# Batch 7 and the last tail with two weighted numerators, batch 1 loaded as fp32, and a new order

## The chip, the cores and the metric

The kernel runs on one core of one Trainium2 chip. The metric is the device time of one execution in microseconds (us). Before the change it is 264.87 us (median of three runs, 264.82 to 264.91). In the text PE is TensorE, DVE is VectorE, ACT is ScalarE, POOL is GpSimd and SP is SyncE; SP only issues transfers (DMAs) here.

## The reference

Attention with a feature map, then a gated MLP with a mixing over positions. There are 8 batches, 8 heads, 576 positions, a head size of 64 and 128 features. Cut to what matters:

```python
def phi(x):                                   # x: q or k, per head
    proj = x @ w_phi                          # 64 -> 128 features
    proj = proj - max(abs(proj), axis=-1)     # m, one number per position and head
    return concat([exp(proj), exp(-proj)])    # 256 features
q_p, k_p = phi(q), phi(k)
num = q_p @ (k_p.T @ v)                       # per batch and head
den = q_p @ k_p.sum(positions) + 1e-6
x   = (num / den)                             # heads side by side: 512 columns
h    = relu(x @ w_in)                         # 512 -> 1024, halves u and v
v_n  = (v - mean(v)) / sqrt(var(v) + 1e-6)    # over the 512 columns
v_s  = w_spatial @ v_n + b_spatial            # over the 576 positions
out  = (u * v_s) @ w_out                      # 512 -> 512
```

As the code has it, the subtraction of m stands ahead of both exponentials: the first half of the features is exp(p - m) and the second is exp(-(p - m)), which is exp(-p + m).

## The kernel before

**Tiling.** Of a batch's 576 positions, 512 are four blocks of 128 and 64 are left over: the tail. The tails of two batches are worked together, as group g for batches 2g and 2g+1. The query side of a batch falls into four units, each of 256 positions and four heads (names with `b.cc.hg`: batch, pair of position blocks, half of the heads); a tail group is one more unit.

**The key side.** k is turned on PE or by a transposing transfer, multiplied by w_phi (`kp`, line 578), DVE takes the maxima of the magnitudes (`km`, line 583), ACT takes both exponentials (`ke`, line 587) and those of the maxima (`kem`, line 592), POOL scales v by them (`vs`, line 633), and PE sums keys times scaled values (`kv`, lines 663 and 665). DVE or ACT copies the sums to SBUF (`kvc`).

**The query side, per unit.** PE multiplies q by w_phi by position (`qp`, line 578); DVE takes the maxima (`qm`, line 583); POOL splits them into two bf16 numbers (`qs`, lines 678 and 679); PE turns them (`qt`, line 683); ACT or DVE copies them (`qc`). Then `qf` makes the features by column: two wide products (line 689), and eight products with a constant `sel` that subtract the maxima in PSUM (line 693). ACT takes exp(p) and exp(-p) of the result (`qe`, line 698). `qn` (line 748) makes 16 short products of 66 columns: both halves of the features accumulate into one sum, whose last columns hold the denominator. DVE takes the reciprocal (`qr`, line 754) and multiplies (`qx`, line 759) into x. The tail's names end in t.

**The MLP.** x is turned (by a transposing transfer `xx` or by PE, `tx`), `vm` and `um` multiply by the two halves of w_in (lines 853 and 921), `vr` and `ur` rectify, `vb` and `va` take mean and variance on DVE, POOL normalizes (`vn`), `sm` mixes positions (lines 935 and 937), `sg` gates on DVE (line 944), `om` multiplies by w_out (line 950), `oc` copies to SBUF and `od` sends the result out.

**The order.** A long string, `ORDER`, lists every step with its engine (`@A` ACT, `@V` DVE, `@P` POOL, `@S` SP, none for PE) and its buffer or PSUM bank numbers. The program is written out in this order, and each engine runs its instructions in it. `warm.n` is n products of the identity (line 365) whose result nobody reads. Batch 0's q and k are loaded as fp32 by SP and ACT and turned on PE; from batch 1 on POOL issues the loads (`lk`, `lq`, lines 398 and 402), which cast to bf16. The functions that would load batch 1 as fp32 (`lkg`, `lqg`) exist, and the list does not use them.

## Time and profile before

The profiled execution took 264.64 us; its span, from the first to the last instruction, is 262.8 us.

| what | us | of the span |
|---|---|---|
| PE busy (weight loads run beside it, 164.0) | 250.8 | 95% |
| DVE busy | 206.6 | 79% |
| ACT busy | 202.2 | 77% |
| POOL busy | 185.1 | 70% |
| first product by w_v starts at | 48.1 | |
| last product by w_out ends, and the last padding starts, at | 258.2 | |
| mean granted clock of TensorE | 1.000 | |

A row of the groups reads: line, engine, operation, tile written and tiles read, shapes, count, then total busy time and the mean duration of one in ns, then the engine's idle time just before them and what ended it. In a table by stage each engine has its busy time in that stretch and, in brackets, the instructions in it. Durations of neighbours on an engine overlap a little, and those of PE a lot: a matmul's row ends long after the next has started.

### The profile page before, as it was taken

To read this page: it belongs to the slowest core of one execution; us is meant where nothing else is said; L and a number is where in the kernel's file an instruction comes from. 1 tells how busy PE (TensorE), PEld (TensorE's weight loads), DVE (VectorE), ACT (ScalarE), POOL (GpSimd) and SP (SyncE) were. 2 spreads that over 40 slices of the span, in tenths; PEclk is the share of its full clock that TensorE was granted. 3 is DMA by queue.
4 is the path that set the end of the run, shared out by engine and by line. 5 is a ranking of instruction groups with operands and counts; after the bars stand their busy time and mean duration, and the time that the engine had idled before them with its cause. 6 is when DMAs were issued, how large, how long until landed. Compare 5 with 4: busy or idle time off the path is not lost.

```text
span 262.8 us, 8513 instructions
## 1 busy us (share of the span) xinstructions
PE 250.8 (95%) x3464; PEld 164.0 (62%) x3499; DVE 206.6 (79%) x362; ACT 202.2 (77%) x330; POOL 185.1 (70%) x338
## 2 busy tenths in 40 slices
PE   7999989999999998989999999999999999999993
PEld 7978768666566565666665766555547586446441
DVE  0679889998899898798899877999987848655730
ACT  3689989999769999999999896997899762453032
POOL 8627996999997996687999992369989820288000
PEclk9999999999999999999999999999999999999999
DMA  7999999962797979998999999998630130044045
GB/s 196 305 193 296 192 203 230 234 75 42 198 209 164 193 123 141 209 143 87 208 205 197 225 107 144 212 197 209 178 127 2 40 84 8 36 159 162 11 148 203
DMA packets 80090, 41.35 MB, mean 157 GB/s; under 512 B 48946, under 2 KB 75442, under 8 KB 80052
## 3 DMA queue, kind: packets, MB, share of 16 engines
q1 hardware_dynamic: 58628, 29.93, 53.1%
q0 software_dynamic: 20592, 10.10, 33.2%
q10 hardware_dynamic: 832, 0.79, 0.9%
q8 instruction: 27, 0.44, 0.7%
q14 instruction: 11, 0.09, 0.1%
HBM read 32.82 MB, written 9.44 MB: 161 GB/s over the span
## 4 chain that ended last, share of the span: by engine, by line
PE 67%; POOL 19%; DVE 5%; DMA 4%; issue 3%; ACT 0%; POOLq 0%; DVEq 0%; ACTq 0%
PE banks L853 10%; PE banks L950 9%; PE banks L935 9%; PE banks L921 8%; POOL vs L633 5%; PE banks L748 5%; PE banks L578 4%; PE banks L663 4%; DMA ld<-in_q_dram 4%; DVE mq L583 3%; PE banks L689 3%; POOL vn L863 2%; POOL vst L645 2%; PE banks L937 2%; PE banks L693 2%
## 5 line engine op out<-in xcount | busy, mean ns | idle before, releaser
L698 ACT ACTIVATE qf<-banks 128x1024 bf16<-128x1024 f32 x72 | 70.1, 1030 | 6.0 <-PE banks L693 5.5
L587 ACT ACTIVATE kf<-banks 128x1024 bf16<-128x1024 f32 x64 | 63.9, 1037 | 5.2 <-PE banks L578 4.8
L633 POOL TENSOR_TENSOR vs<-v,em 128x512 bf16<-128x512 f32 x64 | 65.7, 1043 | 3.0 <-ACT em L592 2.8
L583 DVE TENSOR_REDUCE mq<-banks 128x8 f32<-128x1024 f32 x36 | 43.4, 1220 | 4.1 <-PE banks L578 2.5
L583 DVE TENSOR_REDUCE mk<-banks 128x8 f32<-128x1024 f32 x32 | 38.8, 1218 | 4.5 <-ACT kf L587 2.4
L921 PE MATMUL banks<-xT,w_u 128*128 128x512 bf16 x128 | 32.3, 380 | 0.0
L935 PE MATMUL banks<-w_spT,vn 128*128 128x512 bf16 x116 | 31.6, 379 | 0.7 <-issue 0.2
L853 PE MATMUL banks<-w_v,xT 128*128 128x512 bf16 x118 | 31.2, 379 | 0.5
L950 PE MATMUL banks<-w_out,uT 128*128 128x512 bf16 x113 | 29.6, 379 | 0.7 <-issue 0.2
L277 ACT COPY ob<-banks 128x512 f32<-128x512 f32 x23 | 13.5, 597 | 19.4 <-PE banks L950 18.7
L944 DVE TENSOR_TENSOR uT<-banks,uT 128x512 bf16<-128x512 f32 x32 | 21.4, 683 | 6.4 <-PE banks L937 6.1
L863 POOL TENSOR_SCALAR vn<-vr,mv,rs 128x512 bf16<-128x512 bf16 x32 | 24.4, 767 | 1.2
L663 PEld LDWEIGHTS <-kf 128*128 128x128 bf16 x512 | 21.9, 97 | 4.3 <-issue 0.8
L663 PE MATMUL banks<-vs,kf 128*128 128x66 bf16 x512 | 23.9, 194 | 0.5 <-POOL vs L633 0.3
L875 DVE BATCH_NORM_STATS2 st<-vr 128x6 f32<-128x512 bf16 x32 | 21.5, 683 | 3.5 <-ACT vr L283 3.2
L578 PE MATMUL banks<-wphi,T 64*128 64x128 bf16 x512 | 22.8, 217 | 0.4
L759 DVE TENSOR_TENSOR x<-banks,rc 128x512 bf16<-128x512 f32 x32 | 22.1, 690 | 0.9
L283 ACT ACTIVATE vr<-banks 128x512 bf16<-128x512 f32 (+1 forms) x28 | 16.8, 606 | 7.3 <-PE banks L853 5.8
L748 PEld LDWEIGHTS <-qf 128*128 128x128 bf16 x512 | 19.2, 98 | 4.4 <-issue 0.9
L365 PE MATMUL banks<-ident 128*128 128x128 bf16 x237 | 19.4, 234 | 2.1 <-POOL ident L279 1.7
L665 PE MATMUL banks<-vst,kft 128*128 128x66 bf16 x128 | 21.1, 191 | 0.1
L748 PE MATMUL banks<-kv,qf 128*128 128x66 bf16 x512 | 21.0, 193 | 0.0
(123 smaller groups left out, 481.2 us busy)
## 6 DMA issues: line engine op xcount, KB each, us to landing
v<-in_v_dram SPq DMA_DIRECT2D x16, 512.0 KB, 6.9
out_dram<-ob SPq DMA_DIRECT2D x31, 256.0 KB, 3.0
ld<-in_q_dram POOLq DMA_DIRECT2D x7, 512.0 KB, 10.8
ld<-in_k_dram POOLq DMA_DIRECT2D x7, 512.0 KB, 10.4
uT<-in_q_dram SPq DMA_DIRECT2D x2, 512.0 KB, 5.3
vt<-in_v_dram SPq DMA_DIRECT2D x8, 128.0 KB, 8.6
out_dram<-ob SPq DMA_DIRECT2D x8, 128.0 KB, 3.3
vn<-in_moe_w_spatial_dram POOLq DMA_DIRECT2D x1, 576.0 KB, 7.8
```

What stands on the lines that cost most here:

```text
L578: nc.tensor.matmul(out=bank(banks[y])[:, n * F:(n + 1) * F], lhsT=xT[halves[y], n, :], rhs=wphi[halves[y], :], start=True, stop=True)
L583: nc.vector.tensor_reduce(out=out_, in_=pp.rearrange("p y (n f) -> p y n f", f=F), axis=AX.X, op=ALU.max, apply_absolute_value=True)
L587: nc.scalar.activation(out=kf[:, s].rearrange("p y n f -> p y (n f)"), in_=pp, func=AF.Exp, bias=0.0, scale=(1.0, -1.0)[s])
L633: ENG[e].tensor_tensor(out=get("vs", (b, j))[:, s, :, 0:D], in0=at["v", (b, j // 2)][:, (j % 2) * n:(j % 2 + 1) * n, :], in1=at["em", (b, ...
L663: nc.tensor.matmul(out=pv[:, hh, s, :], lhsT=kf[:, s, c % 2, 2 * hh + c // 2, :], rhs=w[:, s, NB * hh + c, :], start=(c == 0), stop=False)
L698: nc.scalar.activation(out=at["qf", u][:, s].rearrange("p y n t -> p y (n t)"), in_=at["pq", u], func=AF.Exp, bias=0.0, scale=(1.0, -1.0)[s])
L748: nc.tensor.matmul(out=at["pn", u][:, y, n, :], lhsT=f[:, s, y, n, :], rhs=at["kv", b][:, hg * HH + n, s, :], start=(s == 0), stop=(s == 1))
L853: nc.tensor.matmul(out=bank(place)[r], lhsT=lhs[:, kc, r], rhs=w_v[:, kc, :], start=(kc == 0), stop=(kc == KC - 1))
L863: ENG[e].tensor_scalar(out=out_, in0=in_, scalar1=mv, scalar2=rs, op0=ALU.add, op1=ALU.mult)
L921: nc.tensor.matmul(out=bank(place).rearrange("p (c t) -> p c t", c=NB), lhsT=w_u[:, kc, dc * P:(dc + 1) * P], rhs=at["xT", b][:, :, kc, :] ...
L935: nc.tensor.matmul(out=bank(place), lhsT=at["vn", b][:, c, cs], rhs=w_spT[:, c, 0:T0], start=(c == 0), stop=False)
L950: nc.tensor.matmul(out=bank(place), lhsT=at["uT", b][:, dc, c * P:(c + 1) * P], rhs=w_out[:, dc, :], start=(dc == 0), stop=(dc == KC - 1))
```

## The change

Three things change.

- **Batch 7's four units and the last tail group.** The products `qg` are those of `qf` without the eight subtractions, so the exponentials are exp(p) and exp(-p) of the plain projection. `qna` and `qnb` make the sums of either half on its own, in PSUM banks of their own. ACT computes exp(-2m) from the maxima (`qw`), DVE weights the first sum by it (`qy`) and adds the second (`qz`), both over 528 values, and takes the reciprocal from SBUF (`qv`); POOL multiplies into x (`qu`). Numerator and denominator have one common factor less, exp(m), which cancels but for the 1e-6. `qs`, `qt`, `qc`, `qf`, `qn`, `qr` and `qx` of these units go.
- **Batch 1's q and k** are loaded by SP as fp32 (`lkg`, `lqg`, into tiles that the MLP uses later) instead of by POOL as bf16, and its 32 transposes on PE read fp32. The fp32 copy of w_phi now lies in a tile of x.
- **The list `ORDER`** is another one throughout: order, buffer and bank numbers, which engine does a copy or a rectification, and the padding, 237 products before and 211 after.

```diff
-BUFS = dict(ld=3, T=7, ..., mT=4,
+BUFS = dict(ld=3, T=7, ..., mT=4, wq=6, tq=1,
...
+        wq=([P, 2, HH], FP32),
+        tq=([P, 2, HH, DA], FP32),
...
-    wphi_f = const("wphi_f", [D, F], FP32)
+    wphi_f = buf["x"][0][0:D].rearrange("p a h d -> p (a h d)").bitcast(FP32)[:, 0:F]
...
+    def features_u(u, xT):
+        banks = [places.pop(0), places.pop(0)]
+        for y in range(2):
+            nc.tensor.matmul(out=bank(banks[y]).rearrange("p (n t) -> p n t", n=HH), lhsT=wphi[halves[y], :],
+                             rhs=xT[halves[y]], start=True, stop=True)
+        at["pq", u] = pair(*banks)
+
+    def weight(u):
+        nc.scalar.activation(out=get("wq", u), in_=at["mq", u], func=AF.Exp, bias=0.0, scale=-2.0)
...
+    def half_sums(b, cc, hg, s):
+        u = (b, cc, hg)
+        f = at["qf", u]
+        pn = at["pn", u, s] = sums((places.pop(0), places.pop(0)))
+        for y in range(2):
+            for n in range(HH):
+                nc.tensor.matmul(out=pn[:, y, n, :], lhsT=f[:, s, y, n, :], rhs=at["kv", b][:, hg * HH + n, s, :],
+                                 start=True, stop=True)
...
+    def weigh(u, w, r=slice(0, P)):
+        nc.vector.tensor_tensor(out=get("tq", u)[r], in0=at["pn", u, 0][r],
+                                in1=at["wq", w][r].unsqueeze(3).to_broadcast([r.stop - r.start, 2, HH, DA]), op=ALU.mult)
+
+    def join(u, r=slice(0, P)):
+        t = at["tq", u][r]
+        nc.vector.tensor_tensor(out=t, in0=at["pn", u, 1][r], in1=t, op=ALU.add)
+
+    def inverse(u, r=slice(0, P)):
+        nc.vector.reciprocal(out=get("rc", u)[r], in_=at["tq", u][r, :, :, D:D + 1])
+
+    def divide(e, out_, u, r=slice(0, P)):
+        ENG[e].tensor_tensor(out=out_, in0=at["tq", u][r, :, :, 0:D],
+                             in1=at["rc", u][r].to_broadcast([r.stop - r.start, 2, HH, D]), op=ALU.mult)
```

Three places show how the list moves instructions. First, SP's queue from its start; `ob` takes k of batch 0, `uT` its q, `tf` and `vt` the tails, `v` the values, and in the new list `vn` and `xT` take k and q of batch 1. Before:

```order
L382 DMA ob_164<-in_k_dram 128x2x256
L293 DMA tf_77<-in_k_dram 64x8x64 x2
L318 DMA wphi_f<-in_w_phi_dram 64x128
L386 DMA uT_159<-in_q_dram 128x4x256
L386 DMA uT_160<-in_q_dram 128x4x256
L382 DMA ob_166<-in_k_dram 128x2x256
L406 DMA v_75<-in_v_dram 128x4x256
L293 DMA tf_78<-in_q_dram 64x8x64 x2
L293 DMA vt_80<-in_v_dram 64x8x64 x2
L406 DMA v_73<-in_v_dram 128x4x256
```

After:

```order
L385 DMA ob_173<-in_k_dram 128x2x256
L321 DMA x_132<-in_w_phi_dram 64x128
L389 DMA uT_166<-in_q_dram 128x4x256
L389 DMA uT_167<-in_q_dram 128x4x256
L296 DMA tf_78<-in_k_dram 64x8x64 x2
L409 DMA v_72<-in_v_dram 128x4x256
L393 DMA vn_163<-in_k_dram 128x4x256
L393 DMA vn_161<-in_k_dram 128x4x256
L397 DMA xT_137<-in_q_dram 128x4x256
L296 DMA tf_77<-in_q_dram 64x8x64 x2
L296 DMA vt_80<-in_v_dram 64x8x64 x2
L397 DMA xT_136<-in_q_dram 128x4x256
```

Four loads of batch 1 now stand among those of batch 0; the second piece of v (`v_73`) comes after them.

Second, DVE about the first gating products of batch 0, where `TENSOR_SCALAR` is a rectification, `TENSOR_REDUCE` a maximum and `uT` the u half of the MLP. Before:

```order
L754 RECIPROCAL rc_123<-banks 128x8
L759 TENSOR_TENSOR x_127<-banks,rc_123 128x2x256
L279 COPY xT_129<-banks 128x512
L279 COPY xTt_132<-banks 128x4x64
L279 COPY xT_129<-banks 128x512
L583 TENSOR_REDUCE mk_87<-banks 128x2x4
L754 RECIPROCAL rc_124<-banks 128x8
L759 TENSOR_TENSOR x_125<-banks,rc_124 128x2x256
```

After:

```order
L772 TENSOR_TENSOR x_133<-banks,rc_131 128x2x256
L288 TENSOR_SCALAR uT_166<-banks 128x512
L767 RECIPROCAL rc_129<-banks 128x8
L772 TENSOR_TENSOR x_133<-banks,rc_129 128x2x256
L586 TENSOR_REDUCE mq_108<-banks 128x8
L586 TENSOR_REDUCE mk_90<-banks 128x2x4
L288 TENSOR_SCALAR uT_166<-banks 128x512
L873 RECIPROCAL rc_131<-banks 64x8
L282 COPY T_70<-banks 128x512
L288 TENSOR_SCALAR vr_141<-banks 128x512
```

Rectifications that ACT did stand on DVE now. Over the whole list ACT has 13 of the 32 of u instead of 23, and 22 of the 32 of v instead of 25.

Third, the units of batch 7 on DVE. Before:

```order
L759 TENSOR_TENSOR x_127<-banks,rc_123 128x2x256
L279 COPY xTt_132<-banks 128x512
L754 RECIPROCAL rc_122<-banks 128x8
L759 TENSOR_TENSOR x_127<-banks,rc_122 128x2x256
L754 RECIPROCAL rc_124<-banks 128x8
L759 TENSOR_TENSOR x_126<-banks,rc_124 128x2x256
```

After:

```order
L801 TENSOR_TENSOR tq_123<-banks,wq_120 128x528
L985 BN_STATS st_149<-vr_141 128x6
L806 TENSOR_TENSOR tq_123<-banks,tq_123 128x528
L989 BN_AGGR mv_154<-st_149 128x2
L809 RECIPROCAL rc_131<-tq_123 128x8
L282 COPY ob_171<-banks 128x512
L801 TENSOR_TENSOR tq_123<-banks,wq_121 128x528
L806 TENSOR_TENSOR tq_123<-banks,tq_123 128x528
L809 RECIPROCAL rc_130<-tq_123 128x8
```

Each unit has three instructions here where it had two, there is one tile `tq` for all five units, and the product into x stands on POOL.

341 lines of the change are left out of this document (199 added, 142 removed).

## Prediction

> **What bounds the kernel now.** I read the page's head first, then a table by stage that I cut at six places of the program, then the chain of waits.
>
> ```profile
> span 262.8 us, 8513 instructions
> PE 250.8 (95%) x3464; PEld 164.0 (62%) x3499; DVE 206.6 (79%) x362; ACT 202.2 (77%) x330; POOL 185.1 (70%) x338
> ...
> PE 67%; POOL 19%; DVE 5%; DMA 4%; issue 3%; ACT 0%; POOLq 0%; DVEq 0%; ACTq 0%
> ```
>
> ```profile
> core 0: us, PE busy (x) PEld busy (x) DVE busy (x) ACT busy (x) POOL busy (x), PEclk, DMA share, GB/s
> 0.00:37.40 37.40, 34.12 (x546) 29.53 (x547) 25.02 (x35) 28.29 (x48) 28.02 (x55) 1.00 1.16 232
> 37.40:71.30 33.90, 33.16 (x521) 22.35 (x521) 30.69 (x61) 31.49 (x52) 29.83 (x54) 1.00 0.85 153
> 71.30:103.70 32.40, 31.35 (x448) 20.13 (x453) 29.50 (x50) 28.06 (x44) 27.62 (x51) 1.00 1.09 174
> 103.70:136.30 32.60, 31.42 (x483) 19.98 (x486) 28.82 (x49) 30.27 (x50) 26.84 (x50) 1.00 1.08 170
> 136.30:167.20 30.90, 30.16 (x496) 19.85 (x502) 26.43 (x49) 26.88 (x42) 24.06 (x43) 1.00 1.31 176
> 167.20:198.30 31.10, 30.84 (x331) 17.07 (x336) 29.38 (x49) 28.07 (x50) 24.13 (x45) 1.00 0.96 169
> 198.30:258.20 59.90, 59.32 (x654) 34.82 (x658) 36.79 (x76) 28.56 (x47) 24.56 (x45) 1.00 0.26 80
> ```
>
> PE looks busy everywhere, but a matmul's row lasts longer than the time until the next one starts, and the head is padded with products of the identity. So I count what PE is worth by start-to-start times, from merged rows of the chain and the timeline:
>
> ```profile
> 90.43 0.55 PE banks L578 x16
> 116.69 0.57 PE banks L365 x10
> 219.83 1.02 PE banks L748 x32
> 227.78 3.45 PE banks L950 x16
> ...
> 10.88 1.04 PE L509 MATMUL banks<-ident_f,uT 128*128 128x128 f32 x8
> 21.55 1.18 PE L509 MATMUL banks<-ident,ld 128*128 128x128 bf16 x16
> 101.64 0.40 PE L693 MATMUL banks<-mT,sel 64*128 64x128 bf16 x8
> ```
>
> That is 0.034 us for a projection, 0.057 for a padding product, 0.032 for a short product of the sums, 0.216 for a wide one, and about 0.026 for a subtraction product (0.40 less its own length of 0.22, over 7). Counted over the program: 580 wide products 125.3, 1,440 short ones 46.1, 576 projections 19.6, 36 feature stages of about 0.44 each 15.8, transposes and the rest 18.7: **225.5 us** of useful PE work, and 237 padding products, 13.5.
>
> The six cuts lie where PE has 15, 45, 75, 105, 135 and 165 us of useful work behind it. So the first stage took 37.4 us for 15; the five middle ones 160.9 us for 150.3; the last 59.9 us for 60.2, which is PE at its peak. Three regimes follow. In the head PE waits for transfers and for ACT, DVE and POOL. In the middle ACT and DVE are 87 to 95% busy in every stage, and PE loses 10.6 us. From 198.3 on only PE counts: DVE is busy 36.79 of 59.9, ACT 28.56, POOL 24.56.
>
> **The change, part by part.** It rewrites the query path of batch 7 and of the last tail (five units of work), loads batch 1's k and q as fp32, and reorders everything.
>
> *PE.* A unit loses eight subtraction products and one transpose, 8 x 0.026 + 0.057 = 0.27; five units, 1.3 us. Batch 1 gains: its 32 transposes go from bf16 to fp32. The rows above give (1.04 - 0.27)/7 = 0.11 and (1.18 - 0.22)/15 = 0.064, so 32 x 0.046 = 1.5. Useful work stays at 225.5. The gain lies in the PE-bound end, the cost in the head, where PE waits anyway; padding falls from 237 to 211 products, 1.5 us, nearly all of it in the head. If the head had no cover, the 1.5 would be lost.
>
> *The new unit's other engines.*
>
> ```profile
> L759 DVE TENSOR_TENSOR x<-banks,rc 128x512 bf16<-128x512 f32 x32 | 22.1, 690 | 0.9
> L944 DVE TENSOR_TENSOR uT<-banks,uT 128x512 bf16<-128x512 f32 x32 | 21.4, 683 | 6.4 <-PE banks L937 6.1
> L583 DVE TENSOR_REDUCE mq<-banks 128x8 f32<-128x1024 f32 x36 | 43.4, 1220 | 4.1 <-PE banks L578 2.5
> L754 DVE RECIPROCAL rc<-banks 128x8 f32<-128x8 f32 x32 | 6.5, 203 | 5.2 <-PE banks L748 3.1 <-PE banks L683 1.4 <-PE banks L365 0.4
> L633 POOL TENSOR_TENSOR vs<-v,em 128x512 bf16<-128x512 f32 x64 | 65.7, 1043 | 3.0 <-ACT em L592 2.8
> L679 POOL TENSOR_TENSOR mhl<-mq,mhl 128x8 bf16<-128x8 f32 x36 | 7.2, 201 | 3.0
> L678 POOL CAST mhl<-mq 128x8 bf16<-128x8 f32 x36 | 6.9, 191 | 8.6 <-DVE mq L583 8.4
> L592 ACT ACTIVATE em<-mk 128x8 f32<-128x8 f32 x8 | 1.2, 206 | 0.4 <-DVE mk L583 0.4
> ```
>
> DVE did a reciprocal and a product, 0.89. Now it does a weighting and an addition over 528 fp32 values and a reciprocal. The trace shows neither of the two; the nearest row is 0.69 (one PSUM input, 512 values), so I take 0.71 each; below stands 0.68, above the 1.22 of the maximum over 1024 values. Five units: 5 x (0.71 + 0.71 + 0.20 - 0.89) = +3.7 us, up to +8.8. POOL gains the division, as 1.04 (same shapes as the value scaling), and loses 0.39: +3.2. ACT gains 0.21 and loses a copy of about that. All of it falls in the last stage, where these engines are idle for 23 us and more, so I cost it at nothing. From the sums to x a unit's chain grows by 0.71 + 0.71 + 0.20 + 1.04 - 0.89 = 1.8 us; ahead of the exponentials it loses the wait for maximum (1.22), split (0.39) and transpose. If other batches' products did not cover it, what is late next is the transpose of batch 7's x, and 1.8 us is the price.
>
> *The loads.*
>
> ```profile
> 17.30 0.40 PE L509 MATMUL banks<-ident,ld 128*128 128x128 bf16 x4 [0.60 <-DMA ld<-in_q_dram]
> L402 POOL DMA_DIRECT2D ld<-in_q_dram x7 | 7.0, 995 | 2.1 <-PE banks L683 1.8 <-issue 0.3
> ...
> ld<-in_q_dram POOLq DMA_DIRECT2D x7, 512.0 KB, 10.8
> uT<-in_q_dram SPq DMA_DIRECT2D x2, 512.0 KB, 5.3
> ```
>
> Two POOL issues (1.0 each) become four SP issues of 512 KB. They stand on SP ahead of the second half of batch 0's v and behind batch 0's k and q; the v half is wanted by the value scaling only when some 16 us of useful work are done. PE's wait of 0.6 at 17.3 may go: -0.3, from -1.5 (POOL's two issues also count) to +1.5 (the v half or a tail comes late: four transfers of 5.3 us side by side in a stretch that already moves 232 GB/s).
>
> *The new order: the term that decides.* By kinds and engines, I counted what the changed list puts between its own cuts of 15, 45, 75, 105, 135 and 165 us of useful work. A kind's duration is taken start to start, since neighbours overlap:
>
> ```profile
> 248.12 1.91 DVE L944 TENSOR_TENSOR uT<-banks,uT 128x512 bf16<-128x512 f32 x3
> 206.09 3.77 ACT L698 ACTIVATE qf<-banks 128x1024 bf16<-128x1024 f32 x4 [1.60 <-PE banks L693]
> 207.53 4.04 POOL L633 TENSOR_TENSOR vs<-v,em 128x512 bf16<-128x512 f32 x4
> ...
> L283 ACT ACTIVATE uT<-banks 128x512 bf16<-128x512 f32 x23 | 13.7, 611 | 5.4 <-PE banks L921 5.4
> L285 DVE TENSOR_SCALAR uT<-banks 128x512 bf16<-128x512 f32 x9 | 6.1, 682 | 0.7 <-PE banks L921 0.6
> ```
>
> So 0.61 for a gating product, 0.91 for an exponential, 1.00 for a value scaling. For the list of before this gives 142.8 us of DVE in the middle against 144.8 measured (the sum of the five rows), so I scale DVE by 1.014. The changed list moves ten u rectifications net (23 on ACT to 13) and more besides from ACT to DVE. DVE's five loads become **33.7, 28.8, 31.9, 30.0, 28.3**, 152.7 in all: +7.9. ACT's counted load falls from 140.4 to 136.7, POOL's from 137.9 to 137.0; PE's is 150.2. By stage ACT stays or falls but for the third, where it rises from 29.9 to 30.9.
>
> So DVE becomes the fullest engine, and its fill sets the middle. Of before's stages the fullest engine reached 93, 91, 93, 87 and 94% (31.49/33.9 and so on), and the best 20 us were
>
> ```profile
> 160.00:180.00 20.00, 19.79 (x234) 11.20 (x236) 19.28 (x31) 17.57 (x33) 9.39 (x18) 1.00 1.52 197
> ```
>
> 96.4%. A stage takes the larger of DVE's load over its fill and PE's 29.5 to 30.7 over the 0.97 that PE reached at 136 to 198 us. At 96.4%: 35.0 + 30.6 + 33.1 + 31.1 + 30.4 = 160.2, -0.7 against before's 160.9. At 95%: 161.7, +0.8. At 93%: 164.2, +3.3. At 98.5%: 158.3, -2.6. I take 96.4%: where DVE was the fullest by a clear margin (160 to 180) it reached that, and in sum ACT and POOL, for whose results it waits, have less to do. It is the least certain choice here; break-even is near 95.8%.
>
> *The end.*
>
> ```profile
> 258.45 0.59 ACT ob L277
> ...
> L279 DVE COPY ob<-banks 128x256 f32<-128x256 f32 x2 | 0.8, 425 | 3.2 <-PE banks L969 3.2
> out_dram<-ob SPq DMA_DIRECT2D x31, 256.0 KB, 3.0
> out_dram<-ob ACTq DMA_DIRECT2D x2, 128.0 KB, 2.5
> ```
>
> Before, the last product is a whole tile: copy 0.59, transfer 3.0. Now it is half a tile (0.43 or so, 2.5), with a whole one 0.43 us ahead of it whose copy takes 0.68 on DVE: ready 0.3 us earlier than before. -0.3, from -0.5 to 0.
>
> **Sum.** Profiled execution 264.64 (span 262.8 and 1.84 around it): head -0.3, middle -0.7, last stage 0, end -0.3 make 263.3; the median of the runs, 264.87, lies 0.23 above the profiled one: **263.6**.
>
> **Rivals.**
>
> *DVE fills no better than engines did before (slower).* At 93% the middle costs +3.3, less 0.3 at the end: 264.64 + 3.0 + 0.23 = **267.9**. Its place is the stage after 37.4 us, where DVE has 33.7 us to do against PE's 30.5, and the one from 75 us of work on, 31.9 against 30.7. It decides from below 95.8%. For it: three of five stages had their fullest engine at 91 to 93%. Against: there a second engine was about as full, and now DVE stands alone but for the third stage.
>
> [...] Taken as a rival of its own: DVE's fill stays at the middle's 144.8/160.9 = 90%, and 152.7/0.90 = 169.7, +8.8, with the end's -0.3 gives **273.4**.
>
> *It cancels.* DVE at 95%, head and end as forecast: 264.64 + 0.8 - 0.6 + 0.23 = **265.1**. For it: useful PE work is the same to 0.1 us, and so what the rewritten units save comes back as fp32 transposes. That is also the case in which the change doesn't do what it says.
>
> *The stalls vanish.* The 10.6 us that PE loses in the middle come from waits at few places, and a list with only 0.3 us of padding behind the head leaves none planned. DVE at 98.5%, head -0.8: 264.64 - 2.6 - 0.8 - 0.3 + 0.23 = **261.2**. Against: no stage showed any engine but PE above 95%.
>
> **How the numbers follow.** Forecast 0.36, DVE-bound at 93% 0.30, DVE at 90% throughout 0.04, cancels 0.18, stalls vanish 0.12. The forecast's own range, DVE between 95.5 and 97% and the head within half a microsecond, is 262.4 to 264.9. The whole range reaches from a little under the vanished stalls to the DVE-bound case: **260.2 to 268.4**, leaving out the far half of either. A measurement of this kernel can tell 0.2%, 0.53 us. Faster: the forecast nearly whole and the vanished stalls, 0.47; same 0.18; slower 0.35.
>
> **What would show it.** DVE busy about 152 us between 15 and 165 us of useful work, in some 160 us: more than 163 makes the DVE rival right, less than 159 the vanished stalls. The rows for the weighting and the addition should stand near 0.7 and the division near 1.04. The last stage, from 165 us of work to the last product, should take about 60 us; if it takes 62, batch 7's new path is exposed and my zero there is wrong. The first cut should come at 37 us; at 39 the loads were wrong. The end should run 0.3 us shorter behind the last product.

## The result, and the profile after

The changed kernel takes **266.79 us** (median of four runs, 266.37 to 267.65) beside 264.89 for the kernel before on the same chip: a ratio of **1.0076**, 95% interval 1.0051 to 1.0101. It is slower; 263.6 was forecast. Beside the kernels of a later experiment it took 266.88 (266.15 to 268.40; 1.0075, 1.0051 to 1.0099). The kernel before varied by 1.0 us at most on one chip, the changed one by up to 2.3. Medians and ratios, here and below, leave out single executions of a slower state, more than 1.5% above the fastest of the same kernel.

The page's head and its chain of waits, of the changed kernel:

```profile
span 265.0 us, 8426 instructions
PE 254.0 (96%) x3428; PEld 163.8 (62%) x3428; DVE 213.3 (81%) x370; ACT 199.8 (75%) x325; POOL 187.7 (71%) x333
...
PE 77%; DVE 9%; POOL 4%; DMA 3%; issue 3%; ACT 2%; POOLq 0%; DVEq 0%
```

The table by stage, cut where PE has 15, 45, 75, 105, 135 and 165 us of useful work behind it, and at the last product (columns: the stretch, its length, busy time of each engine, granted clock, DMA):

```profile
core 0: us, PE busy (x) PEld busy (x) DVE busy (x) ACT busy (x) POOL busy (x), PEclk, DMA share, GB/s
0.00:36.70 36.70, 34.05 (x471) 28.89 (x471) 24.52 (x33) 27.99 (x50) 28.93 (x59) 1.00 0.98 245
36.70:72.10 35.40, 34.50 (x572) 24.45 (x571) 32.26 (x59) 31.12 (x52) 29.11 (x53) 1.00 1.07 170
72.10:103.50 31.40, 31.27 (x459) 19.63 (x456) 29.33 (x52) 27.89 (x43) 25.25 (x45) 1.00 0.96 150
103.50:136.90 33.40, 32.58 (x472) 19.17 (x470) 30.99 (x55) 31.33 (x49) 28.00 (x51) 1.00 1.13 204
136.90:168.50 31.60, 30.26 (x538) 20.70 (x538) 28.95 (x51) 24.88 (x43) 25.00 (x41) 1.00 1.06 152
168.50:198.70 30.20, 30.18 (x293) 16.04 (x292) 27.71 (x45) 26.09 (x43) 23.98 (x43) 1.00 0.82 172
198.70:259.30 60.60, 60.60 (x638) 34.58 (x637) 39.05 (x80) 30.09 (x52) 27.47 (x45) 1.00 0.27 83
```

Put beside the same cuts of before, the span's 2.2 us come from four places: the head is 0.66 shorter (36.71 against 37.37), the middle 1.04 longer (161.95 against 160.91), the last stage 0.88 longer (60.60 against 59.72), and 0.96 more lies behind the last product (5.72 against 4.76). DVE is the fullest engine in the middle, as forecast, but with 149.2 us and not 152.7. The last stage is PE without a gap.

The middle's 1.04 is what is left of larger losses and gains. By stage, against before: +1.43, −1.05, +0.85, +0.73 and −0.92. The largest loss stands in the first of these stages, 15 to 45 (35.37 against 33.94). There 19 of the changed list's 211 padding products start, and 4 in the old list, which has 10 more in the stage 75 to 105 where the changed list has none. At 0.057 us each, the 15 more would be 0.9 us; that is an estimate, for no run leaves them out.

What PE waited for, longest first (time, times, longest; the start-up wait is left out):

```profile
PE banks L666 <- POOL vs L636: 1.1, 1, 1.1
PE banks L963 <- DMA xT<-x: 0.8, 1, 0.8
PE banks L692 <- DVE kv L282: 0.5, 1, 0.5
```

The same list of the kernel before begins so, and the first row above has its counterpart there in the last, with 0.3 us:

```profile
PE banks L689 <- DVE x L759: 1.0, 2, 0.6
PE banks L509 <- DMA ld<-in_q_dram: 0.6, 1, 0.6
...
PE banks L663 <- POOL vs L633: 0.3, 1, 0.3
```

In the changed kernel the wait for the transfer begins at 109.9 us, ahead of the first w_v product of batch 2 (`vm.2.0`); the one for POOL begins at 141.8, inside the value sums of batch 4 (`kv.4.2`); the one for DVE's `kv` (30.5 to 31.0 us) lies in the head. The new unit's own rows, busy time and mean ns of one:

```profile
L801 DVE TENSOR_TENSOR tq<-banks,wq 128x528 f32<-128x528 f32 x5 | 3.5, 707 | 2.5 <-POOL x L812 1.2 <-PE banks L789 0.7 <-POOL xt L812 0.6
L806 DVE TENSOR_TENSOR tq<-banks,tq 128x528 f32<-128x528 f32 x5 | 3.5, 698 | 0.2
L812 POOL TENSOR_TENSOR x<-tq,rc 128x512 bf16<-128x512 f32 x4 | 4.2, 1044 | 8.0 <-DVE rc L809 8.0
```

### The profile page after: what moved, and what is told of

It is laid out like the page before. It is cut to its first block, busy times and chain, and to the rows that moved or that the text cites. A ratio compares the mean times of both kernels' runs of the same rounds, so it can differ in the third digit from the quotient of the medians.

```text
span 265.0 us, 8426 instructions
## 1 busy us (share of the span) xinstructions
PE 254.0 (96%) x3428; PEld 163.8 (62%) x3428; DVE 213.3 (81%) x370; ACT 199.8 (75%) x325; POOL 187.7 (71%) x333
## 4 chain that ended last, share of the span: by engine, by line
PE 77%; DVE 9%; POOL 4%; DMA 3%; issue 3%; ACT 2%; POOLq 0%; DVEq 0%
PE banks L963 10%; PE banks L1060 9%; PE banks L1031 9%; PE banks L1045 9%; PE banks L581 6%; PE banks L666 5%; PE banks L368 5%; PE banks L761 4%; DMA xT<-x 3%; PE banks L512 3%; PE banks L692 2%; POOL vs L636 2%; PE banks L1047 2%; DVE mk L586 2%; PE banks L696 2%
## 5 line engine op out<-in xcount | busy, mean ns | idle before, releaser
L963 PE MATMUL banks<-w_v,xT 128*128 128x512 bf16 x128 | 32.3, 379 | 0.9 <-DMA xT<-x 0.8
L1045 PE MATMUL banks<-w_spT,vn 128*128 128x512 bf16 x128 | 32.9, 379 | 0.0
L1060 PE MATMUL banks<-w_out,uT 128*128 128x512 bf16 x124 | 30.9, 379 | 0.0
L286 ACT ACTIVATE vr<-banks 128x512 bf16<-128x512 f32 (+1 forms) x27 | 16.1, 602 | 11.7 <-PE banks L963 11.7
L280 ACT COPY ob<-banks 128x512 f32<-128x512 f32 (+1 forms) x24 | 13.6, 582 | 14.4 <-PE banks L1060 6.5
L368 PE MATMUL banks<-ident 128*128 128x128 bf16 x211 | 18.6, 236 | 2.1 <-POOL ident L282 1.7
L772 DVE TENSOR_TENSOR x<-banks,rc 128x512 bf16<-128x512 f32 x28 | 19.2, 686 | 1.5 <-PE banks L368 0.7
L581 PEld LDWEIGHTS <-T 64*128 64x128 bf16 x512 | 15.3, 94 | 8.0 <-issue 5.0
L1031 PEld LDWEIGHTS <-w_u 128*128 128x128 bf16 x128 | 11.6, 98 | 12.7 <-issue 0.6
```

The costliest lines, as they stand in the source:

```text
L368: nc.tensor.matmul(out=bank(place)[:, 3 * P:4 * P], lhsT=ident, rhs=ident, start=True, stop=True)
L581: nc.tensor.matmul(out=bank(banks[y])[:, n * F:(n + 1) * F], lhsT=xT[halves[y], n, :], rhs=wphi[halves[y], :], start=True, stop=True)
L963: nc.tensor.matmul(out=bank(place)[r], lhsT=lhs[:, kc, r], rhs=w_v[:, kc, :], start=(kc == 0), stop=(kc == KC - 1))
L1031: nc.tensor.matmul(out=bank(place).rearrange("p (c t) -> p c t", c=NB), lhsT=w_u[:, kc, dc * P:(dc + 1) * P], rhs=at["xT", b][:, :, kc, :] ...
L1045: nc.tensor.matmul(out=bank(place), lhsT=at["vn", b][:, c, cs], rhs=w_spT[:, c, 0:T0], start=(c == 0), stop=False)
L1060: nc.tensor.matmul(out=bank(place), lhsT=at["uT", b][:, dc, c * P:(c + 1) * P], rhs=w_out[:, dc, :], start=(dc == 0), stop=(dc == KC - 1))
```

## The experiments

All stages, in us, of each kernel's profiled execution by the same cuts of useful work; then the time from the last product to the last landing, from there to the end of the span, the median of the timed runs and the ratio to the kernel before on the same chip.

| kernel | 0–15 | 15–45 | 45–75 | 75–105 | 105–135 | 135–165 | 165–last | to landing | to end | median | ratio, interval |
|---|---|---|---|---|---|---|---|---|---|---|---|
| before | 37.37 | 33.94 | 32.42 | 32.56 | 30.95 | 31.04 | 59.72 | 3.59 | 1.18 | 264.59–264.90 | |
| changed | 36.71 | 35.37 | 31.37 | 33.41 | 31.68 | 30.12 | 60.60 | 4.04 | 1.69 | 266.79 | 1.0076, 1.0051–1.0101 |
| 1 other end | 36.13 | 35.38 | 31.37 | 33.48 | 31.69 | 30.12 | 60.49 | 3.94 | 1.69 | 266.48 | 1.0057, 1.0040–1.0075 |
| 2 old path | 35.95 | 35.38 | 31.37 | 33.44 | 31.68 | 31.08 | 62.39 | 3.22 | 1.69 | 267.39 | 1.0122, 1.0084–1.0159 |
| 3 batch 1 bf16 | 42.54 | 35.20 | 31.17 | 32.31 | 31.54 | 31.42 | 58.42 | 4.42 | 1.24 | 268.35 | 1.0137, 1.0114–1.0161 |
| 4 old split | 39.80 | 37.91 | 33.90 | 34.03 | 31.73 | 32.57 | 61.37 | 4.46 | 1.74 | 279.49 | 1.0552, 1.0535–1.0569 |
| 5 places | 35.55 | 35.38 | 31.37 | 34.04 | 31.44 | 30.11 | 60.61 | 4.58 | 1.69 | 267.28 | 1.0105, 1.0069–1.0141 |
| 6 six transfers | 35.80 | 35.39 | 31.37 | 33.34 | 31.70 | 30.11 | 60.61 | 3.68 | 1.93 | 266.07 | 1.0049, 1.0033–1.0065 |
| 7 before, fp32 | 35.60 | 34.59 | 32.13 | 33.46 | 30.66 | 30.92 | 61.17 | 3.58 | 1.70 | 265.49 | 1.0023, 1.0015–1.0032 |
| 9 changed again | 36.44 | 35.39 | 31.37 | 33.42 | 31.71 | 30.12 | 60.60 | 4.32 | 1.76 | 266.88 | 1.0075, 1.0051–1.0099 |
| 10 DVE relieved | 35.79 | 35.38 | 31.37 | 33.19 | 31.55 | 30.12 | 60.35 | 4.38 | 1.76 | 266.10 | 1.0074, 1.0043–1.0106 |
| 11 POOL relieved | 36.34 | 35.38 | 31.37 | 36.15 | 30.02 | 30.12 | 60.57 | 4.21 | 1.70 | 265.67 | 1.0036, 1.0008–1.0064 |
| 12 ACT relieved | 36.31 | 35.38 | 31.38 | 33.22 | 31.66 | 30.11 | 60.58 | 4.48 | 1.70 | 267.59 | 1.0114, 1.0023–1.0206 |
| 13 all relieved | 36.40 | 35.38 | 31.37 | 36.22 | 29.92 | 30.12 | 60.36 | 4.38 | 1.70 | 265.40 | 1.0038, 1.0009–1.0067 |
| 14 early stores | 35.73 | 35.38 | 31.37 | 32.42 | 31.69 | 30.12 | 60.61 | 4.66 | 1.69 | 266.32 | 1.0072, 1.0045–1.0100 |
| 15 and POOL's order | 36.58 | 35.40 | 31.38 | 32.38 | 30.96 | 30.11 | 60.58 | 4.56 | 1.71 | 264.85 | 1.0005, 0.9993–1.0017 |
| 16 and no fetch | 35.52 | 35.38 | 31.37 | 32.38 | 30.95 | 30.12 | 60.58 | 3.22 | 1.69 | 263.05 | 0.9946, 0.9925–0.9967 |
| 17 no fetch alone | 35.77 | 35.39 | 31.37 | 33.51 | 31.65 | 30.11 | 60.57 | 3.22 | 1.69 | 264.53 | 0.9998, 0.9987–1.0009 |
| 18 and four transfers | 35.13 | 35.39 | 31.38 | 32.38 | 30.94 | 30.12 | 60.58 | 3.28 | 1.06 | **262.34** | **0.9917, 0.9900–0.9934** |
| 19 is 16 again | 36.03 | 35.38 | 31.37 | 32.48 | 30.94 | 30.12 | 60.58 | 3.23 | 1.69 | 262.91 | 0.9934, 0.9920–0.9948 |

The changed kernel, unaltered, was timed again for its spread:

> The changed kernel unaltered, beside the others of this call, for the spread of its times. Theory A (the first stage's loads and the end's transfers vary, the stages between repeat): 265 to 268 us over its runs, with the stages from the first cut to the sixth within 0.05 us of the first profile. Theory B (the stages between vary): some of them differ by over 0.2 us.

Between the first cut and the last product its stages repeat to 0.04 us, and an unchanged piece of list does so to 0.1 us from kernel to kernel. Theory A: only the head and the time behind the last product vary by themselves. So a stage that moves by 0.3 us or more was moved by the edit. The cuts count batch 1's fp32 turns as useful work and the old path's subtractions too, so rows 2, 3 and 7 (226.9, 224.1 and 226.9 us of work where the others have 225.5) are read by their sums and not stage by stage.

### The parts of the change, one at a time (1 to 4 and 7)

The end as before, a whole tile last:

```diff
-oc.7.0:4@A om.7.2:0 och.7.3.0:0@V od.7.0@S odh.7.3.0@A omh.7.3.1 oc.7.2:3@V warm.5:3 och.7.3.1@A od.7.2@S odh.7.3.1@A
+oc.7.0:4@A omh.7.3.1 och.7.3.0:0@V od.7.0@S odh.7.3.0@A om.7.2:0 och.7.3.1@V odh.7.3.1@A oc.7.2:3@A warm.5:3 od.7.2@S
```

> The changed kernel (266.79 us) with one edit at its end: the last whole output tile is multiplied, copied and stored behind the two halves of the split tile, instead of ahead of the second half, so that the last transfer is a whole tile on SP as in the kernel before. All of the computation is done. Theory A (the end was lengthened by what leaves last): the time behind the last product goes from 5.63 us back to about 4.6 us and the kernel to 265.8 us (265.5 to 266.1). Theory B (all transfers of the last microseconds share the bytes in flight, whatever their order): no change, 266.6 to 267.0 us. Theory C (a whole tile is copied and stored later than half a tile): 0.3 us slower, 267.1 us.

5.62 us behind the last product against 5.72: theory A falls. No transfer of PE's instructions (these are told of below) falls among its last stores; in its place the last copy, on ACT, starts 1.06 us behind the last product, where it was 0.45 in the kernel before. The 0.7 us by which this profiled span is shorter is nearly all head (36.13 against 36.71), which the edit does not touch.

Batch 7 and the last tail on the old path (one unit of five shown):

```diff
-qw.7.0.1:0@A
...
-qg.7.0.1:4,5
+qs.7.0.1:0@P
...
+qt.7.0.1:0
+qc.7.0.1:0@A
...
+qf.7.0.1:4,5
...
-qna.7.0.1:4,5 qy.7.0.1:0@V
...
-qnb.7.0.1:4,5
...
-qz.7.0.1@V qv.7.0.1:2@V qu.7.0.1:1@P
+qn.7.0.1:4,5
...
+qr.7.0.1:2@V qx.7.0.1:1@V
```

> The changed kernel (266.79 us) in which batch 7 and the last tail take the old path again: the split on POOL, its transposition, the copy and the four subtracting products come back at 5 units, one weighing by the division's reciprocal in the place of weighting, addition and POOL's division. All else of the list stays. All of the computation is done. Theory A (the new path is exposed and made the last stage 0.76 us longer): 266.0 us, last stage 59.9 us. Theory B (the prediction's: the path is hidden, its term is nothing): 266.6 to 267.0 us. Theory C (the new path saves time that the table's other losses cover): the 20 subtracting products of 0.03 us and the longer chain come back, 267.3 to 268.3 us.

From the first cut to the last product it takes 225.34 us against 222.55: the old path is 2.8 us longer here, 1.4 of it TensorE's own work. I placed its steps by hand, and waits of PE of 0.2 to 0.5 us between them make 1.1, so the rest is an upper bound. Theory C holds by these sums, and the new path is not what made the last stage longer. By the ratios alone (1.0084 to 1.0159 and 1.0051 to 1.0101) the two kernels are not told apart.

Batch 1 by POOL as bf16 again:

```diff
-lkg.0:2@S lkg.1:0@S lqg.0:1@S lqg.1:0@S
+lq.1:2@P lk.1:1@P
...
-lk.3:2@P tq.1.1.1:3
+tq.1.1.1:3 lk.3:2@P
```

> The changed kernel (266.79 us) in which k and q of batch 1 are loaded as bf16 by POOL again, two transfers in the place of four fp32 ones on SP, and turned as bf16. All of the computation is done. Theory A (the fp32 loads made the first stage 0.7 us shorter, as the traces of the two kernels differ): 267.4 us, first stage 37.4 us. Theory B (the shorter first stage comes from the table, and fp32 costs about 0.3 us per turn on PE): 266.0 us or less. Theory C (both cancel): within 0.3 us of 266.8 us.

The first stage becomes 42.5 us. One wait makes most of it, in the changed list:

```profile
PE banks L512 <- DMA ld<-in_k_dram: 3.4, 1, 3.4
```

From the first cut to the last product this kernel is 2.5 us shorter (220.06 against 222.55 for the changed kernel), 1.4 of it the fp32 turns that it saves. Theory A's direction holds, with 6 us in the place of 0.7. The reverse is the old list with the fp32 loads (on the changed kernel's code, with its tiles):

```diff
-lq.1:0@P
...
-lk.1:1@P
...
+lqg.0:1@S lqg.1:2@S
...
+lkg.1:1@S lkg.0:2@S
```

> The kernel before in which k and q of batch 1 stay fp32: four transfers on SP in the place of two converting ones on POOL, and eight turns of fp32. All else of the old list stays. All of the computation is done. Theory A (the fp32 loads make the first stage shorter, and the time of the changed kernel vary from run to run): 263.6 us, with 1 us or more between runs. Theory B (the eight fp32 turns cost 1.4 us of TensorE work, which shows because the stage of batch 1 has no cover): 266.1 us. Theory C (both cancel): 264.4 to 265.2 us.

Ratio 1.0023 (1.0015 to 1.0032), runs between 265.36 and 265.82. The head is 1.8 us shorter, the rest carries the 1.4 us of turns and more, and the last product ends 0.5 later than before. Another 0.5 us appears where nobody looked: from the last landing to the end, 1.70 against 1.18. Its 265.49 us lie between the numbers of theories B and C. Theory A's spread fell, so the fp32 loads alone do not make the changed kernel vary.

The old split between ACT and DVE in the new list:

```diff
-ur.2.3@V
+ur.2.3@A
...
-kvc.4.2@A
+kvc.4.2@V
```

> The changed kernel (266.79 us) in which the 92 rectifications and copies that the new table gives to the other of ACT and DVE go back to the engine that they had in the kernel before; 49 of them leave DVE, 43 leave ACT, and the order of the list stays. All of the computation is done. Theory A (a DVE that is too full set the middle's stages): the middle goes from 162.0 us to about 160.5 us and the kernel to 265.3 us. Theory B (single places, not the load, cost the time): 266.6 us or more, since the list was ordered for the other split.

279.49 us, and the middle 170.1 us with DVE freed. The order was written for its own split; nothing follows on whether DVE is too full, and theory B holds.

### Is an engine too full? (10 to 13)

If the fullest engine sets a stage, taking work from it must shorten the stage. Each of these leaves part of one engine's work out from batch 2 or 3 on; the order stays.

```diff
-        nc.vector.bn_stats(out=get("st", (b, c)), in_=at["vr", (b, c)])
+        w = HALF if b < 2 else HALF // 2
+        nc.vector.bn_stats(out=get("st", (b, c)), in_=at["vr", (b, c)][:, 0:w])
...
-        u = at["uT", b][:, dc, :]
+        w = T0 if b < 2 else T0 // 2
+        u = at["uT", b][:, dc, 0:w]
...
```

> The changed kernel in which DVE does half of two of its works from batch 2 on: the gating product and the norm's statistics take 256 of 512 columns (the other half of the gate and of the statistics is left out). Order and all other work stay. In the stages from 75 to 165 us of useful work (33.4, 31.7 and 30.1 us, 95.2 together) this takes some 10 us from DVE. Theory A (DVE's fullness sets these stages): they become at least 3 us shorter. Theory B (another engine sets them): under 1 us. Theory C (no one engine: each relief gives a little): 1 to 2 us here and in the two runs beside it. The last stage, where TensorE is busy throughout, keeps its 60.6 us by all of them.

```diff
+        m = n if b < 3 else n // 2
-        ENG[e].tensor_tensor(out=get("vs", (b, j))[:, s, :, 0:D],
+        ENG[e].tensor_tensor(out=get("vs", (b, j))[:, s, 0:m, 0:D],
...
```

> The changed kernel in which POOL scales half of the values from batch 3 on (the other half of the scaled values is left out, the sums read what stood there). Order and all other work stay. This takes some 12 us from POOL in the three stages of 95.2 us. Theory A (DVE's fullness sets them): under 1 us shorter. Theory B (POOL sets them, as the stall before the value sums of batch 4 has it): at least 3 us shorter. Theory C (no one engine): 1 to 2 us.

```diff
-        key_exp(at["pk", (b, j)], get("kf", (b, j)), s)
+        kf = get("kf", (b, j))
+        if b < 3 or s == 0:
+            key_exp(at["pk", (b, j)], kf, s)
+        else:
+            nc.scalar.activation(out=kf[:, s, 0].rearrange("p n f -> p (n f)"), in_=at["pk", (b, j)][:, 0], func=AF.Exp,
+                                 bias=0.0, scale=-1.0)
...
```

The queries' second exponential is halved in the same way.

> The changed kernel in which ACT does half of the second exponential of every unit of keys and queries from batch 3 on (the other half is left out). Order and all other work stay. This takes some 12 us from ACT in the three stages of 95.2 us. Theory A (DVE's fullness sets them): under 1 us shorter. Theory B (ACT sets them): at least 3 us shorter. Theory C (no one engine): 1 to 2 us.

> The three reliefs together: what each leaves out is left out here. Useful TensorE work in the three stages is 90 us. Theory A (DVE alone sets the 5.2 us beyond it): no shorter than with the relief of DVE alone, within 0.5 us. Theory C (no one engine): 91 to 92 us for the three stages, more than the sum of the three single gains or near it. Theory D (transfers set them): 94 us or more in all four runs.

The three stages from 75 us of useful work on, as one row of the table by stage: the changed kernel (repeated), then DVE relieved, then ACT relieved.

```profile
103.20:198.45 95.25, 92.00 (x1285) 55.93 (x1298) 87.62 (x149) 82.35 (x131) 77.06 (x134) 1.00 1.01 177
```

```profile
102.54:197.40 94.86, 92.90 (x1301) 55.75 (x1298) 82.56 (x149) 82.36 (x131) 77.04 (x135) 1.00 1.03 178
```

```profile
103.07:198.06 94.99, 92.97 (x1299) 55.85 (x1296) 87.40 (x149) 72.60 (x132) 76.82 (x134) 1.00 1.02 177
```

DVE loses 5.06 us of work, about half of what I had expected to take from it, and the stages 0.39; ACT loses 9.75 and they lose 0.26. By the time as a whole, ACT's relief says nothing (1.0023 to 1.0206); it is read from the stages. **Theory A falls, and with it the model of my forecast for these three stages**: DVE at 92% of them did not set them. With it falls, for the same stages, the rival of DVE at 90% throughout: it was filled to 92%, and 5.06 us less of its work gave 0.39. For the two stages before, of which 15 to 45 holds the largest loss, it was not tried: the reliefs begin with batch 2 or 3, and 15 to 45 takes 35.38 us in all four kernels, with DVE busy for 91% and ACT for 88% of it in the changed one.

POOL's relief (13.9 us of its 77.1) is of another kind, and no theory had it. It shortens one stage alone, 31.68 to 30.02, the one with the stall at `kv.4.2`; with ACT and DVE relieved too it is 29.92, so those add nothing there. With all three relieved these stages take 96.26 us and with POOL alone 96.29: all four kernels stand above 94, which is theory D's number. The stage before that one became 2.7 us longer in this execution, and so with all three reliefs. POOL's freed queue issued its 512 KB of k at 97.8 us instead of 98.7, into the same three stores, which then took 3.6, 7.0 and 8.7 us to land instead of 2.2, 2.7 and 6.3. There PE waited 2.3 us for the transposing transfer, and the granted clock (PEclk) shows what followed:

```profile
108.00:110.00 2.00, 1.50 (x22) 0.77 (x20) 1.97 (x4) 2.00 (x5) 0.50 (x1) 1.00 1.52 92
110.00:112.00 2.00, 0.22 (x1) 0.11 (x2) 0.35 (x1) 1.30 (x2) 1.02 (x4) 1.00 1.13 86
112.00:114.00 2.00, 2.00 (x23) 1.26 (x22) 1.15 (x2) 0.00 (x0) 0.00 (x0) 0.67 1.33 208
114.00:116.00 2.00, 2.00 (x11) 0.90 (x9) 2.00 (x3) 1.51 (x2) 1.38 (x2) 0.50 1.30 130
```

What POOL's relief would save in that stage cannot be read under this wait. So from 75 us of work on two places are left, and neither is an engine's load: a transfer that comes late, and the order on one queue.

### The two places (5, 14 and 15)

My first attempt moved what waits:

```diff
-vm.2.0:2
...
 qp.4.1.0:6,7
...
-vr.2.0:4@V
...
-tqt.1:3 qm.4.1.0:0@V vm.2.2:2
+tqt.1:3 vm.2.0:2 vr.2.0:4@V qm.4.1.0:0@V
...
-kv.3.3:3
+kv.3.3:3 vm.2.2:2
...
-lq.7:1@P
...
-vs.4.2.1@P
+vs.4.2.1@P vsz.4.3@P lq.7:1@P
...
-vsz.4.3@P
```

> The changed kernel with three places of its list mended and nothing else: the first w_v product of batch 2 stands behind two pieces of other TensorE work (it waited for the transfer that transposes x), POOL's load of q for batch 7 (1.00 us on POOL) stands behind the value scaling of batch 4 that it delayed, and the ones column of batch 4's last scaled values is written earlier on POOL. All of the computation is done. Theory A (the middle lost its time at a few places): the stalls of 1.01, 1.24 and 0.56 us at 108.8, 141.5 and 146.9 us shrink to 0.3 us or less each, the middle goes from 162.3 to 160.0 us and the kernel is 2.0 us faster than the changed kernel of the same call. Theory B (DVE's fullness sets the middle): what is mended is waited for a little later; the middle stays above 161.7 us and the kernel gains less than 0.6 us.

No gain: the middle is 162.34. The wait for the transfer went, and four later ones of 0.15 to 0.31 us came in its stead (107 to 118 us), ended by DVE (two), ACT and POOL. At 141 us POOL's value scaling came earlier, but the split of the second tail still stood behind it, and PE waited 1.0 us there. Theory B's number came out; that DVE's load is behind it is not shown, and the 1.0 us at 141 us is POOL's.

The second attempt moved what makes it wait. The transposing transfers of x stand on SP behind three output tiles of batch 0, which leave together though two of them can leave 9 us earlier. SP's issues in the changed kernel (start, time on the queue):

```profile
98.67 1.34 SPq L1071 DMA_DIRECT2D out_dram<-ob  x3
101.42 5.79 SPq L927 DMA_TRANSPOSE xT<-x  x2
```

The third of these stores took 6.0 us to land, 99.57 to 105.53, while POOL's 512 KB of k (8.8 us to land) moved too.

```diff
 xq.5.1:0@S
+od.0.2@S od.0.1@S
...
-od.0.1@S
...
-od.0.2@S
```

> The changed kernel (266.8 us) in which two of the three output tiles of batch 0 that were stored together at 98.9 us leave on SP at about 91 us, when they are ready; nothing else is changed, all of the computation is done. Theory A (the transfer that transposes x for batch 2, issued at 101.2 us behind these 768 KB, is what the w_v product at 108.6 us waits for): its wait of 0.83 us goes to 0.2 us or less, the stage from 75 to 105... that is from 103.2 to 136.6 us goes from 33.4 to 32.5 us, the kernel to 265.9 us and its spread becomes smaller. Theory B (another load sets it, POOL's 512 KB of k that leave at 98.7 us): the wait stays, within 0.3 us of 266.8 us.

```profile
89.58 1.10 SPq L1071 DMA_DIRECT2D out_dram<-ob  x2
...
97.70 0.34 SPq L1071 DMA_DIRECT2D out_dram<-ob  x1
100.45 4.60 SPq L927 DMA_TRANSPOSE xT<-x  x2
```

The wait is gone and the stage takes 32.42 against 33.42: theory A, to a tenth. Its 265.9 us and its smaller spread did not come: the median moved by 0.5 only, to 266.32, and the executions still differ (265.44 to 268.48). At 141 us, POOL's work in the changed kernel stands in this order:

```profile
137.36 1.04 POOL L636 TENSOR_TENSOR vs<-v,em 128x512 bf16<-128x512 f32 x1
138.35 1.00 POOL L405 DMA_DIRECT2D ld<-in_q_dram  x1
139.38 2.05 POOL L636 TENSOR_TENSOR vs<-v,em 128x512 bf16<-128x512 f32 x2
141.37 0.18 POOL L681 CAST mhl<-mq 128x8 bf16<-128x8 f32 x1
141.64 0.20 POOL L682 TENSOR_TENSOR mhl<-mq,mhl 128x8 bf16<-128x8 f32 x1
141.80 1.04 POOL L636 TENSOR_TENSOR vs<-v,em 128x512 bf16<-128x512 f32 x1
142.78 0.19 POOL L681 CAST mhl<-mq 128x8 bf16<-128x8 f32 x1
```

A load's issue of 1.00 us, for data wanted 20 us later, stands in the middle of the value scaling that PE awaits, and the tail's split (142.78) behind it all.

```diff
+qst.2:1@P
 vs.4.3.0:1@P
...
-lq.7:1@P
...
 vs.4.2.1@P
+vsz.4.3@P lq.7:1@P
...
-qst.2:1@P
...
-vsz.4.3@P
```

> The kernel with the early stores, and on POOL, in batch 4, the load of q for batch 7 behind the value scaling, the ones column of the last scaled values and the second tail's split ahead of it. All of the computation is done. Theory A (POOL's order sets the stall at 141 us, as relieving POOL shortened that stage from 31.7 to 30.0 us): 1.0 us or more faster than with the early stores alone, 264.9 us or less. Theory B (the stall only moves to the next thing that POOL does, as it did when the split was left in its place): under 0.4 us.

105–135 takes 30.96 against 31.69, and the median falls by 1.5 us: more than the 1.0 of theory A, though the stage accounts for 0.73, and what remains is not explained; head and end differ from execution to execution. With both mended the middle is **160.2 us**.

### Behind the last product (6, 17, 16, 18 and 19)

Theory: SP looks at the semaphores of the transfers one after the other (in the changed kernel at eight, from 263.00 to 264.03 us), and the four more transfers put the last ones at the front of that row.

```diff
-od.2.2@S
+odh.2.2.0@S odh.2.2.1@S
...
-od.4.2@S
+odh.4.2.0@S odh.4.2.1@S
```

> The changed kernel in which six output tiles of batches 2, 3 and 4, stored in the middle of the program, leave in two halves each: six more transfers on SP ahead of the last ones, the bytes unchanged. All of the computation is done. Theory A (SP looks at eight semaphores of the transfers one after the other at the end; the four more transfers of the change moved the last ones to the front of that row, so that six or seven looks and a pause of 0.4 us stand behind the last landing; six more transfers put them at its end): the time from the last landing to the end of the span goes from 1.7 to 1.1 us, the kernel is 0.6 us faster than the changed kernel of the same call. Theory B (the looks are made while something else ends): no change, within 0.2 us.

Three looks behind the last landing in the place of seven, but with a pause of 0.84 us between the first and the second: 1.93 us, theory A's number missed. It came 0.8 us faster by head and landing, which I cannot put down to the edit.

The landing itself: in the traces PE's instructions come by a queue of their own, 16 KB at a time, one every 230 to 290 instructions near the end (27 in all, for the changed kernel's 3,428 products and as many weight loads).

```
kernel             last product   last 16 KB fetch   took   instructions left   last landing behind the product
before                258.0            243.3         0.88          158                  3.59
fp32 in old list      258.5            243.9         0.96          156                  3.58
old path (2)          261.3            250.0         1.08          124                  3.22
changed               259.3            259.5         1.03            8                  4.04
changed again         259.1            258.3         1.61           23                  4.32
```

The transfers from 256 to 264 us in the changed kernel (queue, packets, MB, share; then issues, their count, KB, median us to landing):

```profile
q8 instruction: 1, 0.02, 0.8%
...
out_dram<-ob SPq DMA_DIRECT2D x4, 256.0 KB, 3.1
out_dram<-ob ACTq DMA_DIRECT2D x2, 128.0 KB, 3.3
```

The experiment takes 34 PE instructions out of the head, so that the last fetch would fall due behind the program's end:

```diff
-warm.8:2
...
-warm.9:2
```

> The changed kernel with only these 17 padding products left out of the head. All of the computation is done. Theory A (the fetch of 16 KB of TensorE's instructions at 258 us, 8 to 23 instructions ahead of its last one, delays the last transfers): no fetch behind 245 us, the time from the last product to the last landing goes from 4.3 to 3.3 us, the kernel from 266.8 to 265.6 us with what the head gains. Theory B (the transfers are late by themselves): no change of that time, and the kernel gains at most the 0.5 us of the head.

> The kernel with the early stores and POOL's order, and two groups of padding (17 products, 34 TensorE instructions) left out of the head. All of the computation is done. Theory A (the three causes add up): 0.5 us from the head, 0.8 us from the end, 263.6 us in all, below the kernel before. Theory B (padding that is left out leaves TensorE slow for longer at the head): no faster than with POOL's order alone.

No such fetch stands behind 240 us in either, and the landing comes 3.22 us behind the last product in both. The same stretch in the kernel with the padding out and nothing else:

```profile
out_dram<-ob SPq DMA_DIRECT2D x4, 256.0 KB, 2.6
out_dram<-ob ACTq DMA_DIRECT2D x2, 128.0 KB, 2.5
```

Theory A: the landing is 1.1 us nearer, the median 2.35 us lower than that of the repeated changed kernel (by the ratios, 0.9998 against 1.0075, 2.0), with 0.67 from the head in the profiled executions. The three mendings together take **263.05** us, 0.9946 (0.9925 to 0.9967): below the kernel before.

The last question was the 0.5 us behind the landing. In four kernels so far it went with the number of transfers: 1.18 and 1.24 without the four fp32 loads, 1.69 and 1.70 with them.

```diff
-od.2.2@S
+odh.2.2.0@S odh.2.2.1@S
...
-od.3.1@S
+odh.3.1.0@S odh.3.1.1@S
```

> The kernel with all three mendings, in which four output tiles of batches 2 and 3 leave in two halves each: four more transfers on SP in the middle, bytes unchanged, all of the computation done. Theory A (SP's looks at the eight semaphores of the transfers are made in a fixed round, and the last transfer's place in it sets how many stand behind the last landing): with four more the last stands at the sixth place of eight as in the kernel before; from the last landing to the end 1.2 us instead of 1.69, 0.5 us faster than the kernel without them. Theory B (the time behind the landing is something else's, the pause of 0.4 us among SP's last instructions): 1.6 us or more, no gain.

> The kernel with all three mendings, unaltered, beside the one with four more transfers. Theory A (its gain is real and steady): 262.8 to 263.5 us, 0.4 to 0.7% below the kernel before. Theory B (the first call caught its lucky runs): 264 us or more.

SP's looks behind the last landing, by their start in us:

```
changed   landed 263.29: 263.31 263.37 263.43 263.49 263.55 263.64 264.03, drains from 264.11, end 264.98
18        landed 259.20: 259.22 259.28 259.35, drains from 259.41, end 260.26
```

Three looks and no pause: 1.06 us. Theory A holds for this kernel. Why six more gave a pause of 0.84 and four more none is open; the pauses of about 0.4 among SP's last instructions move with their place, and I did not find what makes them. The kernel takes **262.34 us**, 0.9917 (0.9900 to 0.9934), the fastest of all; without the four, 262.91 beside it, in theory A's 262.8 to 263.5.

## Why the prediction was wrong, step by step

**The new unit: right.** Weighting 0.707, addition 0.698, division 1.044 were taken as 0.71, 0.71 and 1.04. PE never waits in the last stage, so their cover held as I had said. It took 60.6 us, and not the 62 that would have shown the new path exposed.

**Useful PE work unchanged: 0.9 us off.** I held the last stage at zero because the work was equal. It is PE without a gap in both lists, and takes 60.60 against 59.72. The first thing to suspect is that a unit's sums now come in two groups of eight, where there was one of 16. Counted from the start of a group to the start of what follows, this does not make the 0.9. Before:

```profile
208.31 0.67 PE L748 MATMUL banks<-kv,qf 128*128 128x66 bf16 x16
208.83 0.27 PE L683 MATMUL banks<-ident,mhl 128*128 128x128 bf16 x2
```

After:

```profile
208.45 0.41 PE L789 MATMUL banks<-kv,qf 128*128 128x66 bf16 x8
208.69 0.29 PE L666 MATMUL banks<-vs,kf 128*128 128x66 bf16 x4
```

That is 0.52 us for 16 products and 0.24 for eight, twice 0.24 is 0.48: 0.03 us to a product, as I had priced it. What lies behind the last cut is not the same work in the two lists, though its sum is the same to some tenths: the changed one has 4 more w_u products and 20 more products of value sums there, 32 fewer subtractions and 8 fewer projections. Which of them costs more than its price was not tested, and the cause of the 0.88 stays open.

**The head: right in kind.** −0.3 was forecast within −1.5 to +1.5; −0.66 came in the profiled execution, −0.8 to −1.8 in the others whose head is the same. My "only 0.3 us of padding behind the head" was off: the head runs 187 padding products where it ran 218, but 24 stand behind the first cut (1.4 us), 19 of them in the stage 15 to 45 (1.1 us). The fp32 loads make the head shorter: −1.8 in the old list, and without them the new list loses 6.

**The middle: the step that failed.** "So DVE becomes the fullest engine, and its fill sets the middle" is wrong in its second half: −0.7 us was forecast by it and +1.04 came. DVE was the fullest, with 149.2 us and not 152.7 (92% of the middle). From 75 us of work on its relief by 5 us gave 0.4, ACT's by 10 gave 0.3; the 15 to 45 stage, which lost the most (1.43 us), no experiment relieved, and what sets it stays open, 0.9 us by the estimate being padding. What the runs mended were two places, 1.0 us at a transfer queued behind stores and 0.7 us at an order on POOL's queue, and both were in the list to be read: three stores that leave together, a load's issue amid the scaling. I did read lists by their loads and not by who stands behind whom. The rival of vanishing stalls had the right mechanism ("waits at few places") with the wrong sign: this list brought new ones. The 161.95 us lie between my two signs (159 and 163), so neither of them spoke. With the two places mended the middle is 160.2 us, the very figure that I had worked out from a fill of 96.4%; DVE's fill in it is 149.2/160.2 = 93%, so the agreement is chance.

**The end: −0.3 forecast, +0.96 found.** The step compared copies and last transfers only, and that part was right: where neither cause below is present the end takes 4.34 us (kernel 18) against 4.76 before, −0.4. What it left out: with four more transfers SP looks at seven semaphores behind the last landing in the place of three, 1.69 us in the place of 1.18 (0.5 us), and fewer PE instructions (3,428 products against 3,464, weight loads 3,428 against 3,499) move a 16 KB fetch among the last stores (0.5 to 1.4 us over the 3.22 without it).

**The sum.** The rival of DVE at 93% gave 267.9, the nearest figure to 266.8, for a reason that does not hold from 75 us of work on. The other place that it named, the stage from 15 us of work, is where the largest loss came; DVE was busy for 32.26 of its 35.40 us, and whether DVE set that stage no run shows. The errors against my terms, −0.36, +1.74, +0.88 and +1.26, make the 3.5 us between −1.3 and +2.2 of span. The change's own idea is sound: in the mended list it runs 0.8% below the kernel before.

What stays open: the 9.9 us that PE loses in the middle even so (160.2 for 150.3 of work). Of these, 5.4 lie in the stage 15 to 45 (35.4 for 30), where no experiment acted, 1.1 of them padding. In the three last of its stages, as far as they can be read, the reliefs of all three engines shorten it by no more than 0.4 us beyond POOL's one place, and the traces show the loss as pieces of 0.1 to 0.3 us where products of different kind follow each other (in kernel 16, 0.2 us each ahead of L1045, L1060 and L1127, with nothing in the profile that ends them); that these are unavoidable is argued and not shown.

## What to carry to other kernels

A fill of 90% on an engine does not say that it sets the pace (DVE at 92% of three stages did not set them): take some of its work out in an experiment before believing it. In a hand-ordered program look for the few waits that are new, and move what stands ahead on the queue (a store that was ready long ago, a load wanted much later) and not the one who waits. When an edit changes the number of transfers or of instructions, look behind the last product too: 1.4 us hung on it here.
